# Moving the weights, early tokens and activations of a fused attention and expert kernel to one remainder of 256 bytes

## The chip, the cores and the metric

The kernel runs on one core of a Trainium2 chip, the other cores being idle. The metric is device microseconds (us) of one execution; the median of three runs is quoted. TensorE (PE; its weight loads are shown apart as PEld), VectorE (DVE), ScalarE (ACT) and GpSimd (POOL) are the engines that compute, and SyncE (SP) issues most of the DMAs. Their common working memory, SBUF, has 128 partitions; a tile takes the same byte range of every partition it occupies. "Remainder" below means that start address in a partition, modulo 256.

## The reference

A linear attention feeds a top-1 mixture of experts. Batch is 8, heads 8, sequence 576, head size 64; so there are 4608 tokens of 512 numbers, 8 experts, and a hidden size of 1024. All of it is float32.

```python
q_s = softmax(q, axis=-1); k_s = softmax(k, axis=2)      # with +1e-9 in the sums
x = einsum('bhsd,bhde->bhse', q_s, einsum('bhsd,bhse->bhde', k_s, v))
x = x.transpose(0, 2, 1, 3).reshape(4608, 512)
logits = normalize(x) @ normalize(expert_emb).T / tau
expert, gate = argmax(logits), max(softmax(logits))
out[expert == e] = gate * (relu(x[expert == e] @ w1[e]) @ w2[e])
```

## The kernel before

The work falls into an attention stage over four pairs of batch elements (numbers 0 to 3), whose tokens are routed and scattered by expert to a buffer in HBM, and two kinds of expert slots. The six early slots (0 to 5) work on 256 tokens each, in between the attention's steps; a list of step names, `ORDER`, written out by hand, sets the order in which those steps are emitted. The late slots follow one after the other, each on up to 384 tokens of one expert.

To keep float32 precision, each matmul operand of an expert is split into a high part `h` (rounded, written by ScalarE, line 1130) and a low part `l` (the rest, written by VectorE, line 1132). `ffn1` (lines 1178 to 1180) multiplies a stationary 128x128 block of the first weights by 256 or 384 token columns, three times: `w1h` by `xh`, `w1h` by `xl`, `w1l` by `xh`. ScalarE and VectorE turn the result into `hh` and `hl` (lines 1183 and 1185). `ffn2` (lines 1200 to 1202) takes a 128x128 block of those as the stationary operand and 512 columns of the second weights as the moving one, again three products. Each expert's weights come in four chunks, c = 0 to 3.

Where a tile lies is decided by pools, which place tiles one behind the other in the order in which the program opens them:

- `const` holds small tables, and `wk` the working tiles with their tags. Among the tags of `wk` are `raw` (early weights as they arrive), `et`, and `sn` (a running count of the routing). `h_end`, the fourth chunk of the early activations, is in `wk` too.
- `h_most` holds the other three chunks of the early activations.
- `left` holds two tiles, `left0` and `left1`. At first k, q and v of pair 0 lie in them. Later `weights0` takes the place of `left0`: the early tokens `x`, high and low, then `w1h` and `w1l` of chunks 0 to 2, and `w1h` of chunk 3. `weights1` takes the place of `left1`: `w1l` of chunk 3 and all the second weights.
- `right` holds the later pairs' k, q and v and the token rows, and afterwards, as `late`, the late slots' activations (`h_l`), incoming weights and tokens (`x_0`, `x_1`).

Six small integer tables are counted out by GpSimd (line 257) and converted to float32 by VectorE (line 270); the integers are not used after that.

Of the kernel before, what the change touches and what calls it, by code (L numbers as in the profile page):

```python
# [9 lines left out]
F32 = mybir.dt.float32  # L10
F32R = mybir.dt.float32r
BF16 = mybir.dt.bfloat16
I32 = mybir.dt.int32
# [9 lines left out]
E, F = 8, 1024  # L23
P = 128
NG = B // 2
GT = 2 * S // P
# [21 lines left out]
EARLY_T = EARLY_J * P  # L48
# [12 lines left out]
NF, FC = 4, F // 4  # L61


PAD_LEFT, PAD_RIGHT, PAD_XQ = 24, 184, 48

SCRATCH = 4096

# [65 lines left out]
def attention_moe(ctx, tc, q, k, v, emb, tau, w1, w2, out):  # L133
# [4 lines left out]
    def pool(name, side):  # L138
        return tc.tile_pool(name=name, bufs=1, side=side, reuse_waits="tile")

    const = ctx.enter_context(tc.tile_pool(name="const", bufs=1, side="left"))
    wk = ctx.enter_context(tc.tile_pool(name="wk", bufs=2, side="left"))
# [22 lines left out]
    rooms, att = {}, {}  # L165

    def open_room(name, side):
        rooms[name] = pool(name, side)
        att[name] = rooms[name].__enter__()
        return att[name]  # L170

    def close_room(name):
        rooms.pop(name).__exit__(None, None, None)

    h_end = wk.tile([P, 2, 2, EARLY_T], F32R, tag="h_end", bufs=1, name="h_end")
    h_most = open_room("h_most", "left").tile([P, 6, 2, EARLY_T], F32R, name="h_most")
    KQV = HH * GT * D
    left_of = {}
    left_pool = open_room("left", "left")
    for u in range(2):  # L180
        names = ("v0", "k0", "ve0", "q0") if u == 0 else ("v1", "q1", "k1", "ve1")
        at = 0
        for what in names:
            n = KQV + HH * GT * (what[:2] == "ve")
            left_of[what] = (u, at, n)
            at += n
    left = [left_pool.tile([P, at], F32, tag=f"left{u}", name=f"left{u}") for u in range(2)]
    open_room("right", "right")


# [17 lines left out]
    running = const.tile([P, E], F32, name="running")  # L208
    ints = {}

    def counts(name, shape, pattern, base, by_partition):
        i = const.tile(shape, I32, name=name + "_i")
        f = const.tile(shape, F32, name=name)
        ints[name] = (f, i, pattern, base, by_partition)
        return f

    wtie = counts("wtie", [P, E], [[-1, E]], E, 0)
    base = counts("base", [P, E], [[CAP, E]], 0, 0)

    of_e0 = const.tile([P, 2, E], F32, name="of_e0")  # L220
    exp_i = const.tile([P, E], I32, name="exp_i")
    ints["exp"] = (of_e0[:, 0], exp_i, [[1, E]], 0, 0)
    number = counts("number", [P, EARLY_J * EARLY], [[P, EARLY_J * EARLY]], 0, 1)
    slot_f = counts("slot_f", [NSLOT, 1], [[0, 1]], 0, 1)
    nxt_f = counts("nxt_f", [NSLOT, 2], [[1, 2]], 0, 0)
# [738 lines left out]
    raws, w1h, w1l, w2h, w2l, h_t, xs_t, xg_t, xq_t, fill = [], [], [], [], [], {}, {}, {}, [], []  # L964
    def h_room(m, name, n):

        t = m.tile([P, 2, NC2, n], F32R, name=f"h_{name}")
        h_t[name] = [[t[:, a, 2 * c : 2 * c + 2] for c in range(NF)] for a in range(2)]

    def x_room(m, name, n):  # L970

        t = m.tile([P, 2, NC1, n], F32R, name=f"x_{name}")
        xs_t[name] = [t[:, a] for a in range(2)]
# [31 lines left out]
    def late_room():  # L1005


        close_room("right")
        m = open_room("late", "right")
        h_room(m, "l", T)  # L1010
        r1_all = m.tile([P, NC1, F], F32, name="r1")
        raws.append([r1_all[:, :, c * FC : (c + 1) * FC] for c in range(NF)])
        xg_t[0] = xg_t[1] = m.tile([P, TS, DX], F32, name="xg")
        xq = m.tile([P, TS * DX], F32, name="xq")
        xq_t.append(xq[:, : TS * DM].rearrange("p (n x) -> p n x", x=P))
        DVE.memset(m.tile([P, PAD_XQ], F32, name="pad_xq"), 0.0)
        r2 = [m.tile([P, FC // P, DM], F32, name=f"r2_{c}") for c in range(2)]
        for i in range(2):
            x_room(m, i, T)
        raws.append(r2 + [m.tile([P, FC // P, DM], F32, name=f"r2_{c}") for c in range(2, NF)])  # L1020
        raws.append(r1_all)
        fill.append(wk.tile([P, 2, 2, EARLY_T], F32, tag="h_end", bufs=1, name="fill").rearrange("p a b c -> p (a b c)"))
        DVE.memset(fill_rows(), 0.0)
        DVE.memset(xg_t[0], 0.0)

    def fill_rows():
        return fill[0][:, :DX]
# [241 lines left out]
    h_room_early()  # L1269
    step(NG, "rows", rows_room)  # L1270
    step(NG, "right", late_room)
    def early_slots(s0, n, q, w):

# [35 lines left out]
    for name in ORDER:  # L1309
        if name.startswith("on"):  # L1310
            i, n = name[2:].split(".")[0].split("x")
# [53 lines left out]
    with ExitStack() as ifs:  # L1365
        for s in range(EARLY, SLOTS):
            nxt, i = s + 1, s - EARLY
# [79 lines left out]
```

## Time and profile before

| what | value |
|---|---|
| median of 3 runs | 594.95 us (594.4 to 596.58) |
| the profiled execution | 593.66 us |
| its span, first to last instruction | 591.9 us |
| PE busy | 535.9 us, 91% of the span |
| PEld, DVE, ACT, POOL busy | 80%, 59%, 47%, 35% |
| DMA | 109.23 MB, mean 185 GB/s |
| mean granted TensorE clock | 0.981 of full |

The span leaves 1.8 us outside it. Busy shares are averages over stages with different limits, and a matmul's recorded duration overlaps the next one's, so the starts of matmuls tell their pace better than their durations.

### The profile page before, as it was taken

The page shows a single profiled execution, that of the slowest core. Times are in us where ns is not written, and L with a number is a line of the kernel's source. Part 1 is how long each engine was busy: PE and PEld are TensorE (multiplying, and loading weights), DVE is VectorE, ACT ScalarE, POOL GpSimd, SP SyncE. Part 2 cuts the span into 40 slices and gives each one's busy share as a digit, 9 for nine tenths or more (in the row PEclk, how much of TensorE's full clock was granted, in tenths as well). Part 3 has the DMA queues.
Part 4 walks back from the last instruction along what each step waited for, and adds up shares of the span by engine and source line. Part 5 has one row for each costly group of instructions (what it writes and reads, how often), then busy time and mean ns, then how long its engine had stood idle before and what let it go on. Part 6 is the DMA issues. An engine that isn't in the chain of part 4 may idle for free. (4 is left out here: it accounts for less than half of the span.)

```text
span 591.9 us, 13113 instructions
## 1 busy us (share of the span) xinstructions
PE 535.9 (91%) x5068; PEld 475.7 (80%) x5068; DVE 347.6 (59%) x612; ACT 280.6 (47%) x423; POOL 204.5 (35%) x205
## 2 busy tenths in 40 slices
PE   1587899697899799999999989999999999999995
PEld 0477788586789778898989778889898989989893
DVE  4989989755762545644555647726355372635460
ACT  3459577624666146234354536533435352534350
POOL 1536437765656651571213303030221303031101
PEclk9889999989999899999999989999999999999999
DMA  8956925687554230379978686983756759485100
GB/s 325 403 201 203 319 89 193 207 258 244 187 171 143 83 132 14 115 268 277 307 185 233 166 229 139 252 222 126 177 182 158 199 144 240 130 204 167 38 19 33
DMA packets 65140, 109.23 MB, mean 185 GB/s; under 512 B 9918, under 2 KB 30942, under 8 KB 65056
## 3 DMA queue, kind: packets, MB, share of 16 engines
q1 hardware_dynamic: 55776, 85.76, 49.7%
q0 software_dynamic: 9200, 22.36, 11.0%
q8 instruction: 50, 0.82, 0.6%
q14 instruction: 34, 0.28, 0.2%
q10 hardware_dynamic: 80, 0.02, 0.0%
HBM read 88.66 MB, written 27.33 MB: 196 GB/s over the span
## 5 line engine op out<-in xcount | busy, mean ns | idle before, releaser
L1132 DVE TENSOR_TENSOR weights<-r,weights 128x1024 fp32r<-128x1024 f32 x92 | 113.2, 1246 | 78.0 <-ACT weights L1130 77.1
L1214 POOL DMA_INDIRECT out_dram<-ob,ix x34 | 37.3, 1096 | 251.7 <-ACT ob L1212 227.1
L1130 ACT CAST weights<-r 128x1024 fp32r<-128x1024 f32 x96 | 98.4, 1043 | 19.5 <-DMA r<-in_moe_w_dram 16.7
L1179 PE MATMUL ph<-x,weights 128*128 128x384 f32 (+1 forms) x320 | 103.5, 323 | 2.6 <-issue 2.6
L1178 PE MATMUL ph<-x,weights 128*128 128x384 f32 (+1 forms) x320 | 103.5, 324 | 2.2 <-ACTq L1410 1.3
L1180 PE MATMUL ph<-x,weights 128*128 128x384 f32 (+1 forms) x320 | 103.5, 323 | 0.6 <-DVE weights L1132 0.6
L1200 PE MATMUL po<-weights,h_l 128*128 128x512 f32 x224 | 88.6, 395 | 0.0
L1202 PE MATMUL po<-weights,h_l 128*128 128x512 f32 x224 | 88.5, 395 | 0.0
L1201 PE MATMUL po<-weights,h_l 128*128 128x512 f32 x224 | 88.5, 395 | 0.0
L1185 DVE SCALAR_TENSOR_TENSOR h_l<-ph,h_l 128x768 fp32r<-128x768 f32 (+1 forms) x44 | 37.7, 859 | 52.5 <-ACT h_l L1183 52.2
L1183 ACT ACTIVATE h_l<-ph 128x768 fp32r<-128x768 f32 (+1 forms) x44 | 32.3, 733 | 70.6 <-PE ph L1180 62.1
L1178 PEld LDWEIGHTS ph<-x,weights 128*128 128x128 f32 x320 | 60.9, 190 | 3.5 <-ACTq L1410 1.8
L1179 PEld LDWEIGHTS ph<-x,weights 128*128 128x128 f32 x320 | 60.9, 190 | 3.1 <-issue 2.8
L1180 PEld LDWEIGHTS ph<-x,weights 128*128 128x128 f32 x320 | 60.9, 190 | 1.0 <-DVE weights L1132 1.0
L1178 PE MATMUL ph<-weights 128*128 128x256 f32 x192 | 57.0, 297 | 3.8 <-DVE h_most L1185 3.4
L1179 PE MATMUL ph<-weights 128*128 128x256 f32 x192 | 55.8, 291 | 1.4 <-issue 1.4
L1212 ACT ACTIVATE ob<-po,ix 128x512 f32<-128x512 f32 x34 | 23.3, 685 | 71.1 <-PE po L1202 55.3
L1202 PEld LDWEIGHTS po<-weights,h_l 128*128 128x128 f32 x224 | 42.0, 188 | 10.2
L1201 PEld LDWEIGHTS po<-weights,h_l 128*128 128x128 f32 x224 | 42.0, 188 | 9.7
L1200 PEld LDWEIGHTS po<-weights,h_l 128*128 128x128 f32 x224 | 42.0, 188 | 9.7
L812 POOL DMA_INDIRECT x_by_e<-x,posu x36 | 37.2, 1033 | 26.5 <-issue 9.0
L1180 PE MATMUL ph<-weights 128*128 128x256 f32 x144 | 42.3, 294 | 1.0 <-DVE weights L1132 0.9
(323 smaller groups left out, 951.8 us busy)
## 6 DMA issues: line engine op xcount, KB each, us to landing
r<-in_moe_w_dram SPq DMA_DIRECT2D x96, 512.0 KB, 5.8
k<-in_k_dram SPq DMA_DIRECT2D x6, 1152.0 KB, 12.3
q<-in_q_dram SPq DMA_DIRECT2D x6, 1152.0 KB, 6.6
v<-in_v_dram SPq DMA_DIRECT2D x6, 1152.0 KB, 12.9
xq<-x_by_e SPq DMA_DIRECT2D x36, 192.0 KB, 3.9
left<-in_v_dram SPq DMA_DIRECT2D x2, 1152.0 KB
left<-in_q_dram SPq DMA_DIRECT2D x2, 1152.0 KB, 10.7
left<-in_k_dram SPq DMA_DIRECT2D x1, 1152.0 KB, 7.6
```

Source lines behind the costliest of these rows:

```text
L812: ins = POOL.indirect_dma_start(x_by_e, bass.IndirectOffsetOnAxis(ap=posu[:, c : c + 1], axis=0), buf["x", g][:, j].bitcast(I32), None, bo ...
L1130: ACT.copy(hi, src)
L1132: eng.tensor_tensor(lo, src, hi.bitcast(F32), ALU.subtract)
L1178: PE.matmul(o, w1h[c][:, d, fs], xh[:, d, :n], start=d == 0, stop=False)
L1179: PE.matmul(o, w1h[c][:, d, fs], xl[:, d, :n], start=False, stop=False)
L1180: PE.matmul(o, w1l[c][:, d, fs], xh[:, d, :n], start=False, stop=d == NC1 - 1)
L1183: ACT.activation(hh[c][:, :, :n], ph[:, :, :n], AF.Relu)
L1185: DVE.scalar_tensor_tensor(hl[c][:, :, :n], ph[:, :, :n], 0.0, hh[c][:, :, :n].bitcast(F32), ALU.max, ALU.subtract)
L1200: PE.matmul(po, hh[c][:, u, ts_], w2h[c][:, u, :], start=c + u == 0, stop=False)
L1201: PE.matmul(po, hh[c][:, u, ts_], w2l[c][:, u, :], start=False, stop=False)
L1202: PE.matmul(po, hl[c][:, u, ts_], w2h[c][:, u, :], start=False, stop=c + u == NC2 // 2)
L1214: ins = POOL.indirect_dma_start(out, bass.IndirectOffsetOnAxis(ap=rows, axis=0), ob, None, bounds_check=N - 1, oob_is_err=False,)
```

## The change

Two pads change size and a third is new, `h_end` moves from `wk` to the room of `h_most`, and the six integer tables become slices of one tile that shares the tag `sn`. The core of the diff:

```diff
-PAD_LEFT, PAD_RIGHT, PAD_XQ = 24, 184, 48
+PAD_LEFT, PAD_RIGHT, PAD_XQ, LEFT_PAD = 48, 184, 48, 28
...
-    h_end = wk.tile([P, 2, 2, EARLY_T], F32R, tag="h_end", bufs=1, name="h_end")
-    h_most = open_room("h_most", "left").tile([P, 6, 2, EARLY_T], F32R, name="h_most")
+    h_end = open_room("h_most", "left").tile([P, 2, 2, EARLY_T], F32R, tag="h_end", name="h_end")
+    h_most = att["h_most"].tile([P, 6, 2, EARLY_T], F32R, name="h_most")
...
-    left = [left_pool.tile([P, at], F32, tag=f"left{u}", name=f"left{u}") for u in range(2)]
+    left = [left_pool.tile([P, at + (1 - u) * LEFT_PAD], F32, tag=f"left{u}", name=f"left{u}") for u in range(2)]
...
+    table = wk.tile([P, E * GT], I32, tag="sn", bufs=1, name="table")
+    table_at = [0]
+
+    def tables(shape):
+        first, table_at[0] = table_at[0], table_at[0] + shape[1]
+        return table[: shape[0], first : first + shape[1]]
+
     def counts(name, shape, pattern, base, by_partition):
-        i = const.tile(shape, I32, name=name + "_i")
+        i = tables(shape)
...
-    exp_i = const.tile([P, E], I32, name="exp_i")
+    exp_i = tables([P, E])
...
-        fill.append(wk.tile([P, 2, 2, EARLY_T], F32, tag="h_end", bufs=1, name="fill").rearrange("p a b c -> p (a b c)"))
+        fill.append(att["h_most"].tile([P, 2, 2, EARLY_T], F32, tag="h_end", name="fill").rearrange("p a b c -> p (a b c)"))
```

In the two built programs every engine has the same instructions in the same order with the same waits, apart from the names of the integer tables and the 48 columns in place of 24 of one memset of a pad. What differs is addresses. The start addresses of the tiles that matter:

| tile | before (remainder) | after (remainder) |
|---|---|---|
| `weights0`, `left0` | 60768 (96) | 60640 (224) |
| `weights1`, `left1` | 97792 (0) | 97760 (224) |
| `h_most` | 48480 (96) | 48352 (224) |
| `h_end` | 16544 (160) | 44256 (224) |
| `raw`, `et` and most other tags of `wk` | such as 38560 (160) | such as 34624 (64) |
| `h_l`, `x_0`, `x_1`, late incoming weights | 224 | unmoved |
| `right`: rows and k, q, v of pairs 1 to 3 | 0 to 192 | unmoved |

Inside `weights0`, `weights1` and `late` every piece starts a multiple of 256 bytes behind its tile's start, so it has the tile's remainder. In `left0`, q of pair 0 starts 144 bytes further round (remainder 240 before, 112 after).

## Rows read from the trace of the kernel before

**Rows 1.** The page: span and busy time of the engines.
```profile
span 591.9 us, 13113 instructions
PE 535.9 (91%) x5068; PEld 475.7 (80%) x5068; DVE 347.6 (59%) x612; ACT 280.6 (47%) x423; POOL 204.5 (35%) x205
```
**Rows 2.** Windows: length, busy PE, PEld, DVE, ACT, POOL; granted clock, DMA share, GB/s.
```profile
0.00:50.00 50.00, 26.67 (x590) 21.31 (x590) 38.19 (x84) 25.94 (x38) 20.65 (x52) 0.93 0.78 287
50.00:260.00 210.00, 189.93 (x2784) 167.44 (x2783) 139.04 (x355) 111.56 (x213) 116.00 (x94) 0.98 0.51 171
352.00:586.00 234.00, 231.22 (x1181) 207.25 (x1179) 121.98 (x123) 101.50 (x121) 44.23 (x39) 1.00 0.58 155
```
**Rows 3.** Timeline of PE, a late slot of 384 tokens: start, duration, instruction.
```profile
427.27 0.34 PE L1178 MATMUL ph<-x,weights 128*128 128x384 f32 x1
...
439.95 0.34 PE L1178 MATMUL ph<-x,weights 128*128 128x384 f32 x1
...
444.16 0.39 PE L1200 MATMUL po<-weights,h_l 128*128 128x512 f32 x1
...
460.94 0.34 PE L1178 MATMUL ph<-x,weights 128*128 128x384 f32 x1
```
**Rows 4.** Timeline of PE, first layer of a late slot of 256 tokens.
```profile
312.50 0.28 PE L1178 MATMUL ph<-x,weights 128*128 128x256 f32 x1
...
323.88 0.39 PE L1200 MATMUL po<-weights,h_l 128*128 128x512 f32 x1
```
**Rows 5.** Timeline of PE, first layer of an early slot, chunks 1 to 3.
```profile
160.83 0.28 PE L1178 MATMUL ph<-weights 128*128 128x256 f32 x1
...
166.47 0.28 PE L1180 MATMUL ph<-weights 128*128 128x256 f32 x1
...
167.61 0.28 PE L1179 MATMUL ph<-weights 128*128 128x256 f32 x1
...
170.33 0.27 PE L1151 MATMUL pt<-ident,xge 128*128 128x128 f32 x1
```
**Rows 6.** Groups by line and form: count, busy us, mean ns, idle before.
```profile
L1200 PE MATMUL po<-weights,h_l 128*128 128x512 f32 x224 | 88.6, 395 | 0.0
...
L1178 PE MATMUL ph<-x,weights 128*128 128x384 f32 x224 | 75.8, 338 | 0.8 <-ACT weights L1130 0.8
...
L1178 PE MATMUL ph<-x,weights 128*128 128x256 f32 x96 | 27.7, 289 | 1.3 <-ACTq L1410 1.3
```
**Rows 7.** Windows of the first loads, columns as in rows 2.
```profile
9.50:12.40 2.90, 0.62 (x3) 0.22 (x3) 0.91 (x4) 1.83 (x4) 0.00 (x0) 1.00 1.05 400
12.50:15.40 2.90, 1.15 (x6) 0.65 (x6) 2.82 (x6) 2.70 (x3) 0.00 (x0) 1.00 1.05 394
15.50:18.40 2.90, 0.00 (x0) 0.00 (x0) 2.83 (x5) 2.41 (x2) 0.00 (x0) 1.00 1.04 411
18.50:21.40 2.90, 2.88 (x86) 2.57 (x90) 2.90 (x3) 0.65 (x2) 0.47 (x1) 1.00 1.04 409
```
**Rows 8.** Timeline of DVE, the first k, then k of the second batch.
```profile
4.78 0.69 DVE L364 TENSOR_TENSOR mt<-left 128x512 f32<-128x512 f32 x1 [4.78 <-DMA left<-in_k_dram]
6.95 1.42 DVE L366 TENSOR_TENSOR mt<-mt,left 128x512 f32<-128x512 f32 x2 [1.48 <-DMA left<-in_k_dram]
...
12.57 0.67 DVE L364 TENSOR_TENSOR mt<-left 128x512 f32<-128x512 f32 x1
```
**Rows 9.** Timeline of POOL: pads, first wait, integer tables.
```profile
1.46 0.30 POOL L200 MEMSET pad<- 128x24 f32 x2
...
20.93 8.02 POOL L571 TENSOR_TENSOR x<-left,qmx 128x512 f32<-128x512 f32 x12 [18.69 <-DVE qmx L550]
...
30.08 0.12 POOL L257 IOTA nxt_f_i<- 20x2 int32 x1
```
**Rows 10.** Timeline of DVE, the first conversion of an integer table.
```profile
36.29 0.16 DVE L270 CAST wtie<-wtie_i 128x8 f32<-128x8 int32 x1
```
**Rows 11.** Timeline of DVE, low parts in a late slot.
```profile
441.99 1.23 DVE L1132 TENSOR_TENSOR weights<-r,weights 128x1024 fp32r<-128x1024 f32 x1
...
445.49 1.22 DVE L1132 TENSOR_TENSOR x<-xt,x 128x1024 fp32r<-128x1024 f32 x1 [1.12 <-ACT x L1130]
```
**Rows 12.** Windows in one of the stretches at the lower clock.
```profile
344.10:347.40 3.30, 3.26 (x15) 3.27 (x16) 0.46 (x1) 1.09 (x2) 0.00 (x0) 0.50 1.06 238
```
**Rows 13.** Timeline of PE in that stretch, 256 columns each.
```profile
344.73 0.41 PE L1178 MATMUL ph<-x,weights 128*128 128x256 f32 x1
...
347.08 0.41 PE L1180 MATMUL ph<-x,weights 128*128 128x256 f32 x1
```

## The prediction

> **What bounds the kernel now.** Read the page's busy times first [rows 1]: PE has 535.9 of 591.9 us, far ahead of DVE with 347.6, ACT and POOL. Then cut the span into stages [rows 2]. Up to 50 us the attention's first pair runs, PE is busy for 26.67 us, and DMA and DVE set the pace. From 50 to 260 us the early expert slots fill PE between the attention's steps, 189.93 of 210 us. From 352 to 586 us PE is busy for 231.22 of 234 us, at a granted clock of 1.00, which is the 2.4 GHz level. So in the late slots the time is the number of matmuls by their pace, and only a change of that pace, or an earlier start, moves the end.
>
> The pace is read from starts, since durations overlap. In a late slot of 384 tokens, 96 first-layer matmuls start between 427.27 and 444.16 us [rows 3]: 16.89 / 96 = 175.9 ns each. The 72 second-layer ones up to 460.94 us take 16.78 / 72 = 233.1 ns. In a late slot of 256 tokens, 96 take 323.88 - 312.50 = 11.38 us, 118.5 ns each [rows 4]. The groups give their numbers, each with three lines of equal count [rows 6]: 3 x 224 = 672 of 384 columns, 3 x 96 = 288 of 256, 3 x 224 = 672 of 512. That is 118.2 + 34.1 + 156.6 = 309 us of late matmuls, more than half the span. One nanosecond more on each is 1.6 us.
>
> **The change part by part.** No instruction, order or wait differs, so there are four things to cost: what POOL and DVE do with the tables, the pad, the loads into moved tiles, and the operands that the engines read and write at new remainders.
>
> *Tables and pad.* The two pad memsets take 0.30 us together at 1.46 us; POOL next waits for something until 20.93 us, after 18.69 us of idling [rows 9]. Doubling the smaller memset costs the end nothing; were that cover gone, at most 0.30 us. The last table is counted out at 30.08 us [rows 9] and the first conversion starts at 36.29 us [rows 10]. Even if all conversions had to wait for the last table, 6 us lie between. The tile `sn`, now shared with the tables, is first needed by the routing on DVE, which did the conversions itself long before. Zero.
>
> *Loads.* k, q and v of pair 0 land in the moved tiles. Their order is k of batch 0 (in two parts), k of batch 1, v and q of batch 0, q and v of batch 1. The queue is full, so a window of 2.9 us holds about one load of 1152 KB. v and q of batch 0, at remainders 96 and 240, run at 400 and 394 GB/s; q and v of batch 1, at remainder 0, at 411 and 409 [rows 7]. So a remainder other than zero looks 3 to 4% slower, some 0.1 us for a load, and three loads (k, q, v of batch 1) go from 0 to 224. They are hidden: DVE takes k of batch 1 at 12.57 us without waiting for a DMA [rows 8], and q and v of that batch later still. What lies on the path is k of batch 0, for which DVE idles 4.78 and 1.48 us [rows 8]. It goes from 96 to 224, between the two slower cases, so by 400 against 394 GB/s some 1.5% of less than 6 us of transfer: 0.1 us at most, and as little as 0. I take 0.1. If all three batch-1 loads showed at the end, it would be 0.4 us in all.
>
> [...]
>
> *Operands of DVE and ACT.* In a late slot DVE makes the low part of the second weights from tiles at 224 and 0 in 1.23 us, and that of the tokens from tiles at 160 and 224 in 1.22 us [rows 11]. The pace of this form does not depend on those remainders to 1%, and DVE and ACT are idle nearly half of the late stage [rows 2]: zero, from either side.
>
> *Operands of PE.* This is the term that decides. For moving and stationary operand, today's remainders are 224 and 96 in the late first layer (0 for one third of the stationary blocks of chunk 3, `w1l`), 0 and 224 in the late second layer, and 96 and 96 in chunks 0 to 2 of the early first layer. After the change all are 224 and 224. Per column that is 175.9 / 384 = 0.458 ns for (224, 96) and 233.1 / 512 = 0.455 ns for (0, 224): a moving operand at 0 and one at 224 run within 1% of each other. Chunk 3 of the late slot takes (444.16 - 439.95) / 24 = 175.4 ns, its chunks 0 to 2 (439.95 - 427.27) / 72 = 176.1 ns [rows 3]; the blocks at remainder 0 may be worth 0.7 ns, which the change would give up (168 matmuls, 0.1 us) or spread to the rest (504 matmuls, 0.4 us). The one case of equal remainders is early: 47 matmuls of 256 columns in 166.47 - 160.83 = 5.64 us, 120.0 ns, against 23 of chunk 3 in 170.33 - 167.61 = 2.72 us, 118.3 ns [rows 5], and 118.5 ns late [rows 4]. So equal remainders show no gain, perhaps a loss of 1.5 ns. Signs differ, all sizes are near 1%, and other work runs beside these stretches. I take zero, with -0.4 us below and the rivals above.
>
> *Sum.* 593.66 us (span 591.9 and what lies around it) + 0 + 0.1 + 0 + 0 = 593.8 us for an execution like the profiled one. The median lies 1.3 us above that execution, so I expect **595.0 us**. Its own scatter is the runs' 594.4 to 596.6 and the clock's: in stretches such as 344.1 to 347.4 us the granted clock is 0.50, the 1.2 GHz level, with PE busy throughout [rows 12]. There 256 columns take (347.08 - 344.73) / 11 = 213.6 ns [rows 13] in place of 118.5, so the stretch loses 3.3 x (1 - 118.5 / 213.6) = 1.5 us, and small shifts of the early steps may add or take away one.
>
> **The rivals.**
>
> *Equal remainders collide (slower).* PE fetches the next stationary block while the moving operand streams; if both starting at one remainder makes them meet, the early pair (96, 96) shows the price: 120.0 against 118.5 ns, 1.3%. On the late stage: 288 x 1.5 ns = 0.4 us, 672 x 2.2 ns = 1.5 us, 672 x 3.0 ns = 2.0 us, together 3.9 us, hence 598.9 us. It decides from about 1% of pace on. For it: the only equal pair of today is the slowest per column. Against: the early stretch shares its time with busier DVE and POOL [rows 2], and chunk 3 beside it, with two thirds of its matmuls at equal remainders, runs at 118.3.
>
> *Placement is what holds the pace down (faster).* At the 1.2 GHz level 213.6 ns for 256 columns [rows 13] is a column a cycle, with nothing lost. At twice the clock the pace does not double: 384, 256 and 512 columns would then take 160.0, 106.7 and 213.3 ns, and take 175.9, 118.5 and 233.1. So at 2.4 GHz something other than the array holds the matmuls back, and it may be the way their operands are fetched. The excess is 672 x 15.9 + 288 x 11.8 + 672 x 19.8 ns = 10.7 + 3.4 + 13.3 = 27.4 us. If mismatched remainders caused all of it, the time would fall to 567.6 us; a quarter of it gives 588, and an eighth is enough to be seen. Against: the excess is 9 to 10% for (224, 96) and for (0, 224) alike, and the equal pair (96, 96) has the largest, 12.5%. A cause that lies in the placement should tell these apart.
>
> [...]
>
> *The loads at the start show after all (slightly slower).* 0.4 us by rows, 595.4 us; too small to be told from no change.
>
> **How the numbers follow.** This measurement can tell about 0.5% from no change, 3.0 us, so "same" runs from 592.0 to 597.9 us. My forecast, with the late loads and a clock stretch either way in it, holds 0.79. Collision by over 0.5% gets 0.10: it has one weak row for it. Recovering at least an eighth of the excess gets 0.11: a large prize, with three pairs of remainders against it. The range of 80% is 592.0 to 598.2 us: the unknowns of the forecast (-0.4 and +0.4 us, one clock stretch of 1.5 us, and the runs' scatter of 2.2 us) fill its middle, and its ends reach toward the two rivals.
>
> **What would show it.** Right: late first-layer matmuls still start every 175 to 177 ns, second-layer ones every 232 to 235 ns, 256 columns every 118 to 121 ns; DVE's waits for the first k stay at 4.8 and 1.5 us; the tables cost nothing between 30 and 37 us. Collision: late 384-column starts at 178 ns or more, and 512-column ones at 236 or more. Placement: 384-column starts under 173 ns. The prediction would also be wrong if the early stage ended earlier or later by over 3 us with the pace unchanged, through clock stretches or a shifted wait.

## The result and the profile after

| | before | after |
|---|---|---|
| median of 6 runs each, in one comparison | 595.77 us (594.4 to 600.15) | 588.5 us (585.66 to 591.84) |
| ratio, 95% interval | | 0.9864, 0.9816 to 0.9912 |
| predicted | | 595.0 us (592.0 to 598.2) |
| the profiled execution, its span | 593.66, 591.9 us | 591.84, 590.0 us |

The change saves 7.3 us, 1.2%. The profiled execution of after is the slowest of its six, so the two profiles differ by less than the medians do. They are cut here where the first late slot begins, before it, at the third late slot, and at the last matmul. The rows are windows of before, which the sections above did not show, and then of after (length, busy PE, PEld, DVE, ACT, POOL, granted clock, DMA share, GB/s).

```profile
0.00:278.70 278.70, 235.29 (x3484) 205.13 (x3484) 186.10 (x449) 145.58 (x261) 141.93 (x151) 0.97 0.59 201
278.70:312.50 33.80, 33.80 (x170) 30.50 (x169) 17.06 (x17) 14.37 (x17) 7.62 (x7) 1.00 0.89 242
336.50:358.90 22.40, 18.97 (x120) 17.35 (x120) 11.27 (x12) 8.78 (x12) 3.77 (x4) 0.92 0.77 195
358.90:584.30 225.40, 224.71 (x1152) 202.57 (x1152) 117.13 (x117) 97.68 (x116) 43.91 (x38) 1.00 0.59 158
```

```profile
0.00:285.60 285.60, 236.85 (x3484) 208.24 (x3484) 190.58 (x449) 145.81 (x261) 141.74 (x151) 0.95 0.59 197
285.60:318.70 33.10, 33.10 (x170) 30.22 (x169) 17.08 (x17) 14.39 (x17) 7.73 (x7) 1.00 0.89 241
342.60:361.20 18.60, 17.52 (x121) 16.05 (x121) 11.34 (x13) 8.86 (x12) 3.78 (x4) 1.00 0.93 243
361.20:582.50 221.30, 220.66 (x1151) 201.45 (x1152) 117.10 (x117) 97.69 (x116) 43.91 (x38) 1.00 0.60 161
```

The late slots take 584.3 - 278.7 = 305.6 us before and 582.5 - 285.6 = 296.9 us after, 8.7 us less. One slot, the third, loses 22.4 - 18.6 = 3.8 us of that alone; the others lose 0.4 to 2% each. The early stage, in this execution, takes 6.9 us more, at a mean clock of 0.95 in place of 0.97 and with 4.5 us more of busy DVE. So there are three things to explain: the pace, the third slot, and the early stage.

**The pace.** Timeline of PE after, the slot that answers to [rows 3], then the 256-token slot of [rows 4].

```profile
428.23 0.33 PE L1185 MATMUL ph<-x,weights 128*128 128x384 f32 x1
...
444.90 0.39 PE L1207 MATMUL po<-weights,h_l 128*128 128x512 f32 x1
...
461.26 0.33 PE L1185 MATMUL ph<-x,weights 128*128 128x384 f32 x1
```

```profile
318.78 0.28 PE L1185 MATMUL ph<-x,weights 128*128 128x256 f32 x1
...
330.30 0.40 PE L1207 MATMUL po<-weights,h_l 128*128 128x512 f32 x1
```

384 columns: 16.67 / 96 = 173.6 ns, against 175.9. 512 columns: 16.36 / 72 = 227.2 ns, against 233.1. 256 columns: 11.52 / 96 = 120.0 ns, against 118.5. The granted clock is 1.00 in all these stretches.

The trace gives the clock as a share, not in GHz. At 0.50, 256 columns took 213.6 ns ([rows 13]), 0.834 ns each or 1.2 columns a nanosecond, which is what the prediction's 1.2 GHz stands for; its 2.4 GHz is half that time, 0.417 ns a column, and a cycle there and in the expectations is one such column (32 are 13.3 ns). At 1.00, after the change, 256 columns more take 227.2 - 120.0 = 107.2 ns, 0.419 each. At half of the 213.6 ns for 256 columns, 256, 384 and 512 columns take 106.8, 160.2 and 213.6 ns. After the change 13.2, 13.4 and 13.6 ns come on top, nearly the same whatever their number. Before, the extra grew with the columns: 11.7 ns at 256, 15.7 at 384 and 19.5 at 512.

**The third slot.** Before, then after: SP's issue of the four loads (512 KB each) of the next expert's first weights, then the slot's first, 41st and 42nd matmul on PE.

```profile
335.30 1.89 SPq L1109 DMA_DIRECT2D r<-in_moe_w_dram  x4
336.58 0.36 PE L1178 MATMUL ph<-x,weights 128*128 128x256 f32 x1 [1.34 <-ACTq L1410]
...
341.29 0.28 PE L1178 MATMUL ph<-x,weights 128*128 128x256 f32 x1
344.14 0.58 PE L1179 MATMUL ph<-x,weights 128*128 128x256 f32 x1 [2.57 <-issue]
```

```profile
341.69 1.89 SPq L1116 DMA_DIRECT2D r<-in_moe_w_dram  x4
342.71 0.36 PE L1185 MATMUL ph<-x,weights 128*128 128x256 f32 x1 [1.34 <-ACTq L1417]
...
347.46 0.28 PE L1185 MATMUL ph<-x,weights 128*128 128x256 f32 x1
347.80 0.39 PE L1186 MATMUL ph<-x,weights 128*128 128x256 f32 x1
```

Before, the 42nd matmul starts 2.85 us after the 41st and "issue" means that PE waited for nothing that the profile shows; the stretch at clock 0.50 of [rows 12] begins with that very matmul. After, the same two matmuls are 0.34 us apart and no such stretch follows in this slot. What the profile does show is the transfers. The view by queue has q8, which carries 16,384-byte packets of instructions. These are its rows in windows of before (340.5 to 343 us; from 336.5 to 340.9 us it has no row for q8) and of after (342.6 to 346 us).

```profile
q8 instruction: 1, 0.02, 3.4%
```

```profile
q8 instruction: 1, 0.02, 2.5%
```

In the trace that packet starts 4.5 us after the slot's first matmul before and 2.3 us after it in the changed kernel, and each time PE goes on about 3 us behind it (341.10 to 344.14, 344.96 to 347.80 us). The view does not say whose instructions a packet holds; that these are PE's is read from the moments and tried below.

**The sum.** Second layer: 672 x (233.1 - 227.2) = 4.0 us. Third slot: 3.8 us, of which 0.1 is second layer. First layer: 672 x (175.9 - 173.6) = 1.5 us less, 288 x (120.0 - 118.5) = 0.4 us more. Together 8.8 us, which is the 8.7 us of the late slots.

### The profile page after: what moved, and what is told of

Same layout as the page of the kernel before. It is cut to its first block, busy times and chain, and to the rows that moved or that the text cites. A ratio compares the mean times of both kernels' runs of the same rounds, so it can differ in the third digit from the quotient of the medians.

```text
span 590.0 us, 13113 instructions
## 1 busy us (share of the span) xinstructions
PE 531.2 (90%) x5068; PEld 476.3 (81%) x5068; DVE 352.2 (60%) x612; ACT 281.0 (48%) x423; POOL 204.4 (35%) x205
## 5 line engine op out<-in xcount | busy, mean ns | idle before, releaser
L1139 DVE TENSOR_TENSOR weights<-r,weights 128x1024 fp32r<-128x1024 f32 x92 | 117.3, 1291 | 72.5 <-ACT weights L1137 71.5
L1185 PE MATMUL ph<-x,weights 128*128 128x384 f32 (+1 forms) x320 | 102.3, 320 | 2.3 <-ACTq L1417 1.3
L1187 PE MATMUL ph<-x,weights 128*128 128x384 f32 (+1 forms) x320 | 102.2, 319 | 0.6 <-DVE weights L1139 0.6
L1186 PE MATMUL ph<-x,weights 128*128 128x384 f32 (+1 forms) x320 | 102.1, 319 | 0.1
L1208 PE MATMUL po<-weights,h_l 128*128 128x512 f32 x224 | 87.3, 390 | 0.0
L1209 PE MATMUL po<-weights,h_l 128*128 128x512 f32 x224 | 87.3, 390 | 0.0
L1207 PE MATMUL po<-weights,h_l 128*128 128x512 f32 x224 | 87.3, 390 | 0.0
L1185 PE MATMUL ph<-weights 128*128 128x256 f32 x192 | 58.1, 302 | 3.6 <-DVE h_most L1192 3.3
L1186 PE MATMUL ph<-weights 128*128 128x256 f32 x192 | 56.8, 296 | 1.7 <-issue 1.7
L1187 PE MATMUL ph<-weights 128*128 128x256 f32 x144 | 42.7, 297 | 0.9 <-DVE weights L1139 0.9
## 6 DMA issues: line engine op xcount, KB each, us to landing
v<-in_v_dram SPq DMA_DIRECT2D x6, 1152.0 KB, 13.3
```

The costliest lines, as they stand in the source:

```text
L1139: eng.tensor_tensor(lo, src, hi.bitcast(F32), ALU.subtract)
L1185: PE.matmul(o, w1h[c][:, d, fs], xh[:, d, :n], start=d == 0, stop=False)
L1186: PE.matmul(o, w1h[c][:, d, fs], xl[:, d, :n], start=False, stop=False)
L1187: PE.matmul(o, w1l[c][:, d, fs], xh[:, d, :n], start=False, stop=d == NC1 - 1)
L1207: PE.matmul(po, hh[c][:, u, ts_], w2h[c][:, u, :], start=c + u == 0, stop=False)
L1208: PE.matmul(po, hh[c][:, u, ts_], w2l[c][:, u, :], start=False, stop=False)
```

## The experiments

**One remainder at a time.** Two kernels with the code of after and other pads. The first leaves weights0, h_most and h_end at 96 (as weights0 and h_most are before) and has weights1 at 224; the second has weights0 at 224 and weights1 at 0 (as before).

```diff
-PAD_LEFT, PAD_RIGHT, PAD_XQ, LEFT_PAD = 48, 184, 48, 28
+PAD_LEFT, PAD_RIGHT, PAD_XQ, LEFT_PAD = 16, 184, 48, 60
...
+PAD_LEFT, PAD_RIGHT, PAD_XQ, LEFT_PAD = 48, 184, 48, 36
```

> The changed kernel with weights0 (and the early activations) put back to remainder 96; weights1 stays at 224. Theory A (equality): a matmul takes its columns plus 32 cycles at 2.4 GHz when both operands begin at one remainder, and the old pace otherwise. Then the late second layer (224, 224) keeps 226.7 ns, the late first layer (moving 224, stationary 96) returns to 175.9 ns, and the early second layer (224, 96) to about 233 ns; the time rises by 1.3 us (late first layer: 672 x 2.6 ns slower, 288 x 1.5 ns faster) to 2.9 us over the changed kernel, near 590 to 591 us. Theory B (distance): the same for the late slots, and the early second layer takes a value of its own for distance 128. Theory C (each operand's own remainder, 224 is good): the early second layer lies between 226.7 and 233 ns.

> The changed kernel with weights1 put back to remainder 0; weights0 and the early activations stay at 224. A: late first layer 173.3 ns in chunks 0 to 2, late second layer back to 233.1 ns, early second layer (0, 224) too; the time rises by 672 x 6.4 ns = 4.3 us to 5.8 us over the changed kernel, to 593 or 594 us. B: the same. C: the same late; if only this run loses most of the gain, weights1 carries the gain.

w0_96_w1_224: 587.29 us against 594.84, ratio 0.9874 (0.9808 to 0.9939); late 512 columns every 227.4 ns, 384 every 176.0, no stall in the third slot. w0_224_w1_0: 593.65 us, ratio 0.9972 (0.9936 to 1.0007); 512 columns 233.3, 384 columns 174.2, the stall is there. So the second weights carry the gain, and the first weights add at most what cannot be measured.

**Six more pairs.** The same line again, one execution each. The numbers in a name are the remainders of weights0 (with h_most and h_end) and of weights1. The paces were read, since single times scatter by more than they differ.

```diff
-PAD_LEFT, PAD_RIGHT, PAD_XQ, LEFT_PAD = 48, 184, 48, 28
+PAD_LEFT, PAD_RIGHT, PAD_XQ, LEFT_PAD = 32, 184, 48, 20
...
+PAD_LEFT, PAD_RIGHT, PAD_XQ, LEFT_PAD = 8, 184, 48, 28
...
+PAD_LEFT, PAD_RIGHT, PAD_XQ, LEFT_PAD = 56, 184, 48, 4
...
+PAD_LEFT, PAD_RIGHT, PAD_XQ, LEFT_PAD = 40, 184, 48, 52
...
+PAD_LEFT, PAD_RIGHT, PAD_XQ, LEFT_PAD = 24, 184, 48, 20
...
+PAD_LEFT, PAD_RIGHT, PAD_XQ, LEFT_PAD = 64, 184, 48, 4
```

> weights0 and early activations at 160, weights1 at 128, late tiles at 224. A: late first layer 175.9 ns, late second layer 233.1 ns, early second layer (128, 160) about 233 ns, early first layer (160, 160) 120.0 ns. B: late first layer (distance 64) and second layer (distance 160) take values of their own, possibly below 173.3 and 226.7 ns. C: as A.

> weights0, early activations and weights1 all at 64, late tiles at 224: equal early, unequal late. A: early second layer (64, 64) 226.7 ns and early first layer 120.0 ns, late first layer 175.9, late second layer 233.1 ns. B: the same early; late values of their own for distance 160 and 96. C: early second layer about 233 ns, since neither operand is at 224.

> weights0 and early activations at 0, weights1 at 160, late tiles at 224. A: late first layer 175.9, late second layer 233.1 ns, like every unequal pair. B: values of their own for distances of 224 (first layer) and 192 (second layer, 64 apart).

> weights0 and early activations at 192, weights1 at 32, late tiles at 224. A: late first layer 175.9, late second layer 233.1 ns. B: values of their own for distances of 32 (first layer) and 64 (second layer).

> weights0 and early activations at 128, weights1 at 96, late tiles at 224. A: late first layer 175.9, late second layer 233.1 ns. B: values of their own for distances of 96 (first layer) and 128 (second layer).

> weights0 and early activations at 32, weights1 at 192, late tiles at 224. A: late first layer 175.9, late second layer 233.1 ns, even for the second layer's nearest unequal neighbour (32 apart). B: values of their own for distances of 192 (first layer) and 224 (second layer).

Late 512 columns, with h_l at 224: 234.2, 233.4, 233.3, 229.0, 232.9 and 233.1 ns in that order. None reaches 227.3; weights1 at 32, that is 64 bytes past 224, is the one that stands out. In w0_64_w1_64 the early second layer has both operands at 64 and runs near 227 ns for h_end while its late one, 64 against 224, takes 233.4: it is the distance between the operands that counts, not where one of them lies. Times, 596.64 and 593.12 us for the first two, against 594.84; the other four came from a slower chip (604.44, 603.76, 604.52, 608.35 us against 608.77).

**Equality at zero.** After, with h_l and weights1 at 0, and the first weights and the tokens at 224.

```diff
-PAD_LEFT, PAD_RIGHT, PAD_XQ, LEFT_PAD = 48, 184, 48, 28
+PAD_LEFT, PAD_RIGHT, PAD_XQ, LEFT_PAD = 48, 184, 40, 36
```

> After, with the late activations h_l and the second weights at remainder 0, and first weights, early and late tokens at 224. Theory (only the distance between the two operands counts): late 512-column starts every 227.3 ns as in after, 384 columns 173.5, time as after, 587 to 589 us. Rival (it is the remainder 224 that is good for an operand): 233 ns and 592 to 595 us.

227.5 ns for 512 columns, 586.14 us against 594.48, ratio 0.9868 (0.9808 to 0.9927). The rival falls.

**The operands alone.** The kernel that computes nothing of the reference.

```diff
+    for r in range(REPEATS):
+        if r:
+            DVE.tensor_tensor(zero, zero, po[bank], ALU.max)
+            for _ in range(150):
+                DVE.tensor_tensor(low, raw[:, 0], raw[:, 1], ALU.subtract)
+        for n in (256, 384, 512):
+            for m in moving:
+                bank = (bank + 1) % 4
+                some(m, n, bank, 48)
```

> This kernel computes nothing of the reference: it loads the first weights of one expert, makes rounded copies of them, and runs 48 matmuls of one form after the other, with the stationary blocks at remainder 128 and the moving operand at eight places: 0, 32, 64, ... 224 bytes further on (128, 160, 192, 224, 0, 32, 64, 96), with 256, 384 and 512 columns; first with the other engines idle, then once more with VectorE subtracting float32 tiles beside it. Theory (the distance between the moving and the stationary operand's start, modulo 256, sets the pace, and nothing else is needed): at distance 0 starts every N columns + 32 cycles, 120.0, 173.3 and 226.7 ns; at 64 near 229 ns for 512 columns; at the other distances 233 ns for 512, 173 to 176 for 384, 117 to 119 for 256, in both halves alike. Rival (the operands collide with what ScalarE, VectorE or the DMAs write or read at those remainders): in the quiet half all eight distances run within 1 ns of each other, and only the second half tells them apart.

Timeline of PE, 512 columns in the quiet half, 48 matmuls a row, move_a to move_h at distances 0, 32, ... 224; then the first rows of 512 columns in the second half, and DVE's row beside it.

```profile
135.36 11.04 PE L61 MATMUL po_b<-move_a,still 128*128 128x512 f32 x48
146.24 11.37 PE L61 MATMUL po_c<-move_b,still 128*128 128x512 f32 x48
157.44 11.16 PE L61 MATMUL po_d<-move_c,still 128*128 128x512 f32 x48
168.44 11.37 PE L61 MATMUL po_a<-move_d,still 128*128 128x512 f32 x48
179.65 11.36 PE L61 MATMUL po_b<-move_e,still 128*128 128x512 f32 x48
190.85 11.40 PE L61 MATMUL po_c<-move_f,still 128*128 128x512 f32 x48
202.09 11.35 PE L61 MATMUL po_d<-move_g,still 128*128 128x512 f32 x48
213.28 11.35 PE L61 MATMUL po_a<-move_h,still 128*128 128x512 f32 x48
224.47 5.91 PE L61 MATMUL po_b<-move_a,still 128*128 128x256 f32 x48
...
336.96 11.04 PE L61 MATMUL po_b<-move_a,still 128*128 128x512 f32 x48
347.84 11.37 PE L61 MATMUL po_c<-move_b,still 128*128 128x512 f32 x48
```

```profile
225.28 188.96 DVE L72 TENSOR_TENSOR low<-raw 128x1024 fp32r<-128x1024 f32 x150
```

Each row's start to the next, over 48: 10.88 / 48 = 226.7 ns at distance 0, 11.20 / 48 = 233.3 at 32, 11.00 / 48 = 229.2 at 64, and so on. With DVE busy it is again 10.88 / 48. All sizes, by such differences (256 columns from the second half, since the first row of the first half begins slowly, 7.98 us for its 48):

| distance in bytes | 0 | 32 | 64 | 96 | 128 | 160 | 192 | 224 |
|---|---|---|---|---|---|---|---|---|
| 256 columns, ns | 119.8 | 117.9 | 117.7 | 119.8 | 118.8 | 118.5 | 117.7 | 118.3 |
| 384 columns, ns | 173.3 | 173.3 | 173.5 | 176.5 | 176.0 | 173.8 | 174.6 | 174.0 |
| 512 columns, ns | 226.7 | 233.3 | 229.2 | 233.5 | 233.3 | 234.2 | 233.1 | 233.1 |

Nothing but the two operands is needed for differences of this size, and the rival falls. Only the moving operand was shifted here; that the distance counts, and not its own place, is shown by the kernels above. The table gives before's late layers too: distance 128 and 384 columns, 176.0 (175.9 there); distance 32 and 512 columns, 233.3 (233.1). At 512 columns the late second layer of every kernel here is within 1 ns of it.

At 384 columns the distance modulo 256 is not the whole rule. Timeline of PE in w0_64_w1_64, the first layer of two late slots running:

```profile
427.21 0.34 PE L1185 MATMUL ph<-x,weights 128*128 128x384 f32 x1
...
443.86 0.40 PE L1207 MATMUL po<-weights,h_l 128*128 128x512 f32 x1
...
460.66 0.34 PE L1185 MATMUL ph<-x,weights 128*128 128x384 f32 x1
...
477.62 0.40 PE L1207 MATMUL po<-weights,h_l 128*128 128x512 f32 x1
```

16.65 / 96 = 173.4 ns and 16.96 / 96 = 176.7 ns: the slots take turns, as their tokens lie in x_0 or x_1, both at remainder 224. w0_192_w1_32 does the same. And in w0_224_w1_0 chunk 3, two thirds of it at distance 0 and one third at 224, takes 4.24 us for 24 matmuls, 176.7 ns, more than either distance alone (173.3 and 174.0). What else counts there, no run separates.

**The pads alone.** Before, with two pads: h_end stays in wk and the tables in const, weights1 goes to 224. The first weights move too, from 96 to 64 (distance 160 in the first layer).

```diff
-PAD_LEFT, PAD_RIGHT, PAD_XQ = 24, 184, 48
+PAD_LEFT, PAD_RIGHT, PAD_XQ, LEFT_PAD = 16, 184, 48, 4
...
-    left = [left_pool.tile([P, at], F32, tag=f"left{u}", name=f"left{u}") for u in range(2)]
+    left = [left_pool.tile([P, at + (1 - u) * LEFT_PAD], F32, tag=f"left{u}", name=f"left{u}") for u in range(2)]
```

> Before, with other pads alone, so that the second weights lie at 224 like the late activations, the early tokens and first weights at 64; h_end and the integer tables stay where they were in before. Theory (equal remainders in the second layer carry the gain): late 512-column starts every 227.3 ns, 384 columns near 174.8, the stall of 2.85 us in the third late slot gone, 587 to 588 us, ratio 0.987. Rival (the tables or h_end have a share in it): 589.5 us or more with the same pace.

585.57 us against 594.48, ratio 0.9861 (0.9808 to 0.9914), 512 columns 227.2 ns, 384 columns 173.6, no stall. Two lines of the diff give all of the change's gain; the tables and h_end's new room have no part in it that can be measured. Since the first layer became faster here as well, it is w0_96_w1_224, with the first layer at its old 176.0 ns, that shows the second weights to carry most of it.

**The loads of the third slot.** First a failed try: the four loads of the next expert's first weights are written behind the slot's first layer.

```diff
-                    gn[4][7]()
+                    if i != 2:
+                        gn[4][7]()
...
+                        if x and i == 2:
+                            gn[4][7]()
```

> Before, with all addresses as they were; only the four loads of the next expert's first weights in the third late slot are issued after its first layer in place of ahead of it. Theory (the stall of 2.85 us in that slot is a code load that queues behind those four loads, and the stretch at the lower clock after it comes of the stall): pace as before (233 ns for 512 columns), stall and stretch gone, 590 to 591.5 us. Rival (the stall has another cause, or hangs on the placement itself): stall and stretch stay, 594 to 596 us. A third outcome: the later loads are themselves late, PE waits in the fourth slot, 595 us or more.

Time unchanged (ratio 1.0, 0.997 to 1.0031), stall 2.75 us. But it tells nothing, because SP waits for nothing of the first layer: the loads were issued 1.4 us ahead of the slot's first matmul (337.72 against 339.1 us), as before (335.30 against 336.6). The second try holds them by three small transfers to the same place, each of which waits for the one ahead.

```diff
             e = expert()
+            if i == 3:
+                for _ in range(3):
+                    SP.dma_start(r1_all[:QB, 0, F - 8 :], w1f[:QB, :8])
             for c in range(NQ):
```

> Before, with all addresses as they were and three small transfers, each waiting for the one ahead, put on SP's queue in front of the next expert's first weights in the third late slot; they hold those four loads (and the second weights behind them) back by some 5 to 6 us. Theory (the code load of PE in that slot queues behind these loads): the 16,384-byte code packet starts 1 to 2.5 us after the slot's start in place of 4.5, the stall of 2.85 us falls under 0.5 us and the stretch at the lower clock behind it is gone; what the time does then hangs on whether the loads still arrive in time: 590 to 592 us if they do, more if the fourth slot waits for them. Rival (the code load is asked for late by PE's side): packet at 4.5 us, stall 2.6 to 2.9 us, 594 us or more.

SP's queue in that kernel (start, time, transfers), the row of q8 from 333.5 to 336 us, and the slot's window:

```profile
332.18 4.52 SPq L1110 DMA_DIRECT2D r<-in_moe_w_dram  x3
338.29 2.15 SPq L1112 DMA_DIRECT2D r<-in_moe_w_dram  x4
```

```profile
q8 instruction: 1, 0.02, 2.8%
```

```profile
333.50:351.70 18.20, 17.23 (x121) 15.80 (x121) 11.33 (x13) 8.95 (x12) 3.65 (x4) 1.00 0.75 171
```

The four loads now go out 4.8 us after the slot's start, the code packet starts 0.7 us after it, PE does not stall, the clock stays at 1.00 and the slot takes 18.2 us in place of 22.4, with all addresses and the pace (233.2 ns) as before. The median is 591.1 us against 595.13, ratio 0.9951 (0.9924 to 0.9978); the profiled execution, 586.51 us, is the fastest of its seven. So the loads issued ahead of the packet made the stall: with the packet at 0.7 us in place of 4.5 it was gone, and the stretch behind it too.

The other profiles agree. In the nine with a second-layer pace of 232.9 ns or more and the loads where they were, the packet starts 4.5 to 4.6 us into the slot, two matmuls start 2.6 to 3.0 us apart, and a stretch at 0.50 begins within 1.5 us of the second. In w0_192_w1_32 (229.0 ns) the two figures are 3.9 and 1.9 us, with no stretch. In the seven near 227 ns they are 2.1 to 2.3 us and at most 0.5 us, again with no stretch in this slot. But in two of those seven, after_again and first_layer_64, 3.4 us at 0.50 come in the fourth slot instead, which then takes 35.6 us in place of after's 34.0. So the 2.5 us of the stall are won each time, the 1.5 us of the stretch not. Why a faster second layer gets the packet through 2.3 us earlier, with loads issued at nearly the same moment of the slot (1.3 us ahead of it before, 1.0 us after), is not shown.

**The early stage.** The changed kernel once more, and after with a gap of 192 bytes in weights0.

> The changed kernel unaltered, for its early stage. If the later end of its early stage (first late slot at 285.7 us) was chance, it is now within 2 us of before's 278.8 and the median is 585 to 587 us; if it belongs to the change, it is again 283 us or later and the median 588 to 590 us.

```diff
-    def in_left(u, parts):
+    def in_left(u, parts, gap=0):
...
-            where.append(t[:, i * n : (i + 1) * n].rearrange("p (a b) -> p a b", a=a))
+            at = i * n + (gap if i >= 2 else 0)
+            where.append(t[:, at : at + n].rearrange("p (a b) -> p a b", a=a))
```

> After, with a gap of 192 bytes in weights0, so that the first weights begin at remainder 160 and the tokens stay at 224 (distance 64 in the first layer, 0 in the second). Theory (distance alone): 256 columns every 117.8 ns in place of 119.9, 384 columns 173.4, 512 columns 227.3 as in after; by 288 late and some 576 early matmuls that is at most 0.6 + 1.2 us, ratio to before 0.984 to 0.988, not to be told from after with certainty. Rival (equal remainders are best everywhere): 256 columns no faster than 119.5 and 384 columns at 175 or more, time as after or above.

after_again: 588.32 us against 595.13, ratio 0.9873 (0.9847 to 0.9898); in its profile, again the slowest of its runs, the first late slot starts at 284.1 us. By the expectation the later end belongs to the change; but with before's own addresses that slot starts at 275.7 us in held_loads and 281.2 us in later_loads, so a part of it may still be chance. first_layer_64: 583.53 us, ratio 0.9799 (0.9779 to 0.9820), the fastest kernel here; 256 columns every 117.7 ns, 384 every 173.9, 512 every 227.4. The pace explains 288 x 2.2 + 576 x 2.1 ns = 1.8 us of the 4.8 us between the two; the rest lies in its early stage, which ended at 276.2 us, at a mean clock of 0.96 in place of 0.94. Besides the clock, one row stands out there. DVE and POOL near 93 us, before and then after:

```profile
93.41 3.38 POOL L1132 TENSOR_TENSOR weights<-r,weights 128x1024 fp32r<-128x1024 f32 x1
92.73 1.79 DVE L1132 TENSOR_TENSOR weights<-r,weights 128x1024 fp32r<-128x1024 f32 x1
```

```profile
94.56 2.42 POOL L1139 TENSOR_TENSOR weights<-r,weights 128x1024 fp32r<-128x1024 f32 x1
96.91 2.14 POOL L566 TENSOR_TENSOR qd<-q,qmx 128x1152 f32<-128x1152 f32 x1
98.98 2.05 POOL L797 TENSOR_TENSOR nrm<-ssall,half 128x4 f32<-128x4 f32 x1
93.86 6.29 DVE L1139 TENSOR_TENSOR weights<-r,weights 128x1024 fp32r<-128x1024 f32 x1
```

Before, POOL's subtraction takes 3.38 us (its other three 2.39 to 2.41) and DVE's 1.79 us; after, POOL's runs through in 2.42 us and DVE's lasts 6.29, until POOL is in the third instruction. It does so in four profiles: after (both times), h_l_0_w1_0 and w0_224_w1_0. All have weights0 at 224 and the working tiles at 64. No other profile of these kernels has it; first_layer_64, whose working tiles are at 64 too but whose first weights are at 160, shows 2.04 us. Two kernels move the working tiles alone, after's to 160 and before's to 64:

```diff
-PAD_LEFT, PAD_RIGHT, PAD_XQ, LEFT_PAD = 48, 184, 48, 28
+PAD_LEFT, PAD_RIGHT, PAD_XQ, LEFT_PAD = 8, 184, 48, 28
...
+    between = att["h_most"].tile([P, 40], F32, name="between")
```

```diff
+    between = att["h_most"].tile([P, 24], F32, name="between")
...
-    for m, n in ((const, PAD_LEFT), (att["right"], PAD_RIGHT)):
+    for m, n in ((att["right"], PAD_RIGHT),):
```

> After, with 40 columns less of the pad in const and 40 columns of pad ahead of h_end, so that the working tiles of wk (raw among them) and the tables behind the pad lie at the remainders they have in before (raw at 160 in place of 64), and h_end, h_most, weights0, weights1 exactly where they are in after. Theory (the working tiles at 64 let POOL shut DVE out): the subtraction of DVE at 93 us takes 1.8 us, POOL's beside it 3.4, the early stage ends 3 to 4 us earlier, 584 to 585.5 us. Rival (weights0 at 224 or the exact moment is what counts): 6.3 us again, 587.5 to 589 us.

> Before, with the 24 columns of the pad in const put ahead of h_most instead, so that the working tiles of wk, h_end among them, move from 160 to 64 and the tables behind the pad with them, and h_most, weights0 and weights1 stay where they are. Theory (the working tiles at 64 let POOL shut DVE out): the subtraction of DVE at 93 us takes 6.3 us in place of 1.8, 597 to 599 us. Rival (weights0 at 224 or the exact moment is what counts): 1.8 us, 594.5 to 596 us.

DVE's instruction takes 1.79 us in after_raw_160 and 1.80 in before_raw_64. Ratios: 0.9893 (0.9845 to 0.9941) and 1.0007 (0.9979 to 1.0035), on a chip where before takes 602.55 us. So neither the working tiles at 64 nor weights0 at 224 does it by itself; every kernel whose first weights lie at 224 and whose working tiles lie at 64 shows it, and no other. Taking it away brought no gain that can be measured, and h_l_0_w1_0, where the instruction lasts 6.34 us, starts its first late slot at 279.7 us, near before's 278.8. Both theory and rival fail in part; what decides between DVE and POOL, and how much of the later early stage comes of it, stays open.

## Why the prediction was wrong

**What bounds the kernel** was right: the late slots are PE's pace, and the pace is what changed.

**Tables and pad, zero:** right. The six tables took 0.55 us of POOL from 29.69 us on, and DVE's first conversion came at 36.35 us (36.29 in [rows 10]).

**Loads, 0.1 us:** right. The windows of [rows 7] fell from 400, 394, 411 and 409 to 392, 389, 390 and 392 GB/s, most where the remainder went from 0 to 224. DVE's first waits were 4.78 and 1.36 us (4.78 and 1.48 in [rows 8]), and k of the second batch was taken at 12.62 us (12.57).

**Operands of DVE and ACT, zero:** right for the late stage, where the low part of the weights took 1.23 us again ([rows 11]). In the early stage one DVE instruction grew by 4.5 us, through POOL beside it. I had looked at late rows only, where the two hardly meet.

**Operands of PE, zero: this step failed.** It compared paces per column, 0.458 ns for (224, 96) and 0.455 for (0, 224), and read from them that remainders make no difference. But these were two unequal pairs, and both are among the slow ones: 176.0 and 233.3 ns in the table of the operands alone. Of the equal pair it had one row, with 256 columns, and took from it "no gain, perhaps a loss of 1.5 ns". That row was read rightly, and it holds after too (120.0 ns). What was missed is that the extra of an equal pair hardly grows with the columns: 13.2, 13.4 and 13.6 ns at 256, 384 and 512 columns after the change, while that of before's late pairs is 11.7, 15.7 and 19.5. So equal remainders are among the worst at 256 columns and the best at 512. 120.0 ns at 256 columns, taken as 13.2 ns over the columns, would have given 173.4 and 226.8 ns for the late slots, and 672 x 2.5 + 672 x 6.3 - 288 x 1.5 ns = 5.5 us of gain. Dividing by the columns hid it.

**The rivals.** "Placement is what holds the pace down" had the mechanism: of its excess of 27.4 us the late layers gave back 4.0 + 1.5 - 0.4 = 5.1 us, some 19%. The argument against it, that equal and unequal pairs lose alike, rested on the same division: the equal pair's 12.5% was at 256 columns, where the unequal pair of [rows 4] has 11.8 of 106.7 ns, 11.1%, and not 9 to 10%. That a quarter of the excess would have given 588 us, and the median is 588.5, is luck: 3.8 us came from the third slot, and the early stage took some back. Even equal remainders leave 13.2 to 13.6 ns over the columns, and what takes them no run shows. "Equal remainders collide" is true at 256 columns alone, 0.4 us. That the fetch of the next block meets the moving operand was the author's guess: with DVE idle, the pace of 512 columns in operands_alone goes from 226.7 to 234.2 ns with the distance of the two start addresses, but whether and where the two reads meet, no run shows.

**Missed altogether:** the stall and the stretch behind it, 3.8 us of the 8.7 us that the late slots gave in the profiled executions. The stretch was in the prediction ([rows 12], at 1.5 us) and was put down to chance; the gap of 2.85 us right ahead of it was not asked about.

**The marks.** By its own marks, 384 columns at 173.6 ns fell between "right" (175 to 177) and "placement" (under 173); 512 columns at 227.2 was outside every band it had named. The early stage ended 6.9 us later in the profiled execution, but not with the pace unchanged, as its last mark wanted.

## What to carry to other kernels

Where matmuls run one behind the other with a new stationary block each, put the start of the moving and of the stationary operand at the same remainder of 256 bytes if the moving one has 512 columns of float32 (226.7 ns here, against 229.2 to 234.2 at other distances); with 256 columns another distance is a little better (117.7 against 119.8), and at 384 the runs leave part of it open. Compare paces by what they take over their columns, in ns, at each size, before dividing by the size. When a stretch at the lower clock stands in a busy stage, look at the matmul ahead of it: a gap that "issue" ends (2.57 us of it here) may come of the kernel's own loads ahead of a packet of instructions, and holding those loads back for some 6 us removed both here.

## What the runs showed of the hardware

- The pace of these matmuls depends on the distance of the operands' starts modulo 256, by up to 7.5 ns of 227 (operands_alone, 512 columns: 226.7 ns at 0, 234.2 at 160), in steps that differ with the number of columns; at 384 columns two tiles of the same remainder gave 173.4 and 176.7 ns (w0_64_w1_64); at a granted clock of 0.50, 256 columns took 213.6 ns ([rows 13]), against 118.5 at 1.00.
- A 16,384-byte code packet that starts 4.5 us into a slot, behind four loads of 512 KB, went with a stall of PE of 2.85 us; with the loads held back by 6 us the packet started at 0.7 us, PE did not stall, and no wait for the loads showed.
- DVE and POOL, each subtracting 128x1024 from SBUF at the same time, took 1.79 and 3.38 us, or 6.29 and 2.42, with the same instructions in the same order. DVE's form takes 1.23 us where POOL has no instruction beside it ([rows 11]). DVE had started first both times, 0.7 us ahead, so the order of the starts does not decide which of the two is held up; what does, and where they meet, no run here settles.
